# A planned order of an attention and FFN kernel: two units share one step of exponentials

## The chip, the cores and the metric

The kernel runs on one core of one Trainium2 chip. TensorE (PE) multiplies, VectorE (DVE), ScalarE (ACT) and GpSimd (POOL) do the rest, SyncE (SP) issues the DMAs. The metric is the time of one execution on the device, in microseconds, as the median of several runs.

## The reference, cut to what matters

```python
q, k, v: (8, 8, 576, 64); omega: (128, 64); w_in: (512, 2048); w_out: (2048, 512)
def phi(x):                                   # x is q or k, scaled by 64 ** -0.25
    h = x @ omega.T - sum(x * x) / 2
    return exp(h - max(h, axis=-1)) / sqrt(128)
kv  = einsum('bhsm,bhsd->bhmd', phi(k), v);  z = phi(k).sum(axis=2)
att = einsum('bhsm,bhmd->bhsd', phi(q), kv) / (einsum('bhsm,bhm->bhs', phi(q), z) + 1e-6)
x   = att.transpose(0, 2, 1, 3).reshape(4608, 512)
h   = x @ w_in
out = (0.5 * h * (1 + erf(h / sqrt(2)))) @ w_out
```

## The kernel before

**Units.** Attention is cut into 32 units: batch b (0 to 7) and a pair of heads j (0 to 3), unit number 4b + j. A unit projects its k and q (2 x 576 rows of each, 18 tiles of 128 columns: tiles 0 to 8 are k's, 9 to 17 q's), subtracts maxima, takes exp, forms the product of exp(k) with v (`kv`, or `kv_split`), brings exp(q) into the transposed form and divides (`num`, `den`, `rcp`, `div`). There are three kinds. Units 0 to 3 (mode 0) take exp tile by tile out of PSUM, with the maxima as a bias (`exp_tiles`). Units 4 to 7 (mode 1) subtract the maxima on DVE into an array of 128x2304 fp32 in SBUF (`shift_tiles`) and take one exp over it (`exps`). Units 8 to 31 (mode 2, "split") project in fp32r with high and low parts (`x_high` on ACT, `x_low` on POOL, `proj` and `proj_q` on PE, `proj_add` and `q_blocks` on DVE), subtract, and take one exp over the array too. A unit of modes 0 and 1 multiplies in fp32.

**The step of exponentials.** A split unit's step is one exp over 2304 columns, then a gelu of a single element. That gelu makes ACT load gelu's table back at once, since the gelus of the FFN follow; so a step has two loads of tables. There are two such arrays, `et` and `et2`. Split units with an even number above 8 use `et2`, all others of modes 1 and 2 `et`, so successive units take turns. What is written before the step is `split_pre`, what follows it `split_post`. In the order's list an option `pair`, 0 in this kernel, lets a unit on `et2` take the next unit with it.

**The FFN** works on 13 blocks of tokens (256, 256, ten of 384, 256). Block 0 is in fp32. Later blocks split x, the weights and the gelus into fp16 high and low parts, three products for one (`mm1`, `mm2`); from block 4 on the first product uses seven products of sums of quarter blocks in place of eight (`w_prod`), the second `w_mm2`. The weights are loaded as 16 pieces (w_in first), rounded (`w_hi`, `w_lo`, `w_shift`, `w_round`), their absolute maximum is taken (`w_abs` on ACT, `w_max` on DVE), and when the maximum of all of w_in is known (`wchain_a` to `wchain_f`, with two small products on PE, L559 and L565) they are scaled and split. The raw pieces have two buffers. PSUM has eight banks: three for accumulators of the second product, five shared by attention and the first product.

**Products of zeros.** At the start PE runs 22 products of zeros (`warm`), and eight groups of four more (`hold`, L448) stand in the order at places of their own.

**The order.** `op(engine, cost, function, ...)` notes every operation with what it reads and writes. ORDER is a list written out by a search, of numbers of operations with letters for the PSUM banks that each takes; `Planner.run` issues them in this order, and every engine keeps its own part of it strictly. So an engine that waits holds all that is behind it in its queue, SP's loads too.

Of the kernel before, what the change touches and what calls it, by code (L numbers as in the profile page):

```python
# [19 lines left out]
P = 128  # L20
# [8 lines left out]
X = dict(plain=8, kvp=8, eb0=8, ttr=1, pair=0, amax=63, qm=1, xm=0, km=0, prelu=1, n0=4, vs=5,  # L29
# [5 lines left out]
14 0 1 15 49 2a 12 17caa 50 22g 18 52dfa 57b 19 20 9h 4e 21 11 23 55 5e 24 58 59 56 7c 159 25hg 16 28 160 29 26 51 60ec 161  # L35
27 30aa 53 35ha 6b 3f 165 61 119 63 84 86 39f 54 85 31 64 62 65ga 70ba 162 166 40 37c 36 72f 38 71 66 167 87ada 32 73 168 90
120 92h 41cg 93 88 74b 94 67 42 43 75 95hf 163 89 44 122eba 96 171 123 169 33 657 91 172 45ca 98 8d 177 46 97 47 100ga 127h
48 76ca 101 174 99 34 105fa 128 173 658 125 107g 124 178 77 129 179 126 10d 78 106 130dh 108 79 80ec 180 175 68 133 131 81
170 181 121 660baa 132 164 82 183 663 83 661 109f 135ga 665c 664 110 662 184 666 186 176 189 667 111df 112 668cb 136 69 102
134 113 140ga 190 669 191 144a 185 693 142e 114 145 659 192 115hd 671 187 195 143 670 672 103 141 673 146ge 116 117 137 193  # L40
118 196 198 147 679aa 680 674ca 104 148 197 199 149 188 138 696baa 675 699 182 150gh 681c 201 139 300a 301 302 202 204 203
# [12 lines left out]
999 786 996a 1004 392 1000 393 417 527 409 429 1005 988 992 801 530b 997 656 394 1009 967 789b 802 528 405 397 531 432 1010
790 803 993 435 529 436 1001b 1006c 998 804 1002 1011aa 1013 532 536a 1012 1014 1007 1017 437 276 537 533 438 805 968 972
1003 439 277 395 538 534 539 535 793ab 794 795 540 542c 544b 545 806 543b 550 970 442 440 541 546 441 444 969 1021 807 445
796 552a 551 448 553 1018 554 809 443 811 1022 1008 547 1073 548 555 449 549 446 1015c 1019b 1075 556 1023a 450 560b 447 974
557 558 561 1080 398 451 1016 1024 452 971 1020 562 563 559 568a 566 564 569 565 797ca 453 1076 567 1081 570 576b 813 1025
454 574 577 1026 1085 1027 1028 461 457 973 571 810 455 578 798 1029 456 812 1030 572 575 975 582 459 579 580 573 1031 1032
976 799 583 1033 462 584a 1086 585 586 590 1036 581 977 458 800 460 591 1040 587 1707 1074 598 1059 588 592b 593 1037 594 399  # L60
1038 595 1077ba 1044 1042 1078 1041 1090 1039 1045 463 589 599 1082c 596 1043 464 1091 1095 1087a 1079 1083 1088 597 1100 465
1101 606 600a 1084 978 466 601 602 979 1092b 608b 1096 1089 1062 607 603 1164 1093 1104 980 1097c 1102aa 604 1094 605 1108
609 610 981 614 1105 1112 1098 1109 616a 1113 467 1034 1099 611 1103 617 618 1035 472 1110c 1106a 1111 1114b 612 615 815 1166
1116 622 613 1167 619 1115 1107 1046caa 1060 620 1171 468 1047 624b 1048 623 1176 625 1049 1117 470 1050 621 1172 1051 1168aa
1173b 1169 1118 474 626 1181 630 1174 396 1177 631 638 469 1052 1170 814 632a 1119 1178a 1709 1053 1175 1186 1165 471 1182
627 1056 1120 1183c 633 634 639 628 1061 1187 1125 629 1191 475 1179 1054 1184 1195 473 640b 641 1255 635 1192 1180 1063
1188a 1121 636 1193ba 1199 1189 476 1055 1185 1203 642 816 477 637 646 647 648 643 478 1122 1200 1204 1190 1194 1123 817a
1201a 644 645 1202 818 479 1196 1124 649 1064 650 1126 819 1129 1130 1205a 820 1206 1197c 1257 653 485 823b 1133 1135 1127
1065ab 1131 480 1258 1198 824 486 821 1066 825 822 651 1150 829a 481 826 487 835a 1262 1267 1128 1067 1134 827 1068 1208 836c
1263 830 483 1136 831 654 1209 1259aa 828 1069cb 1057 1132 1272 484 837b 832 838b 482 1268 844 1153 839 1260 488 489 490 1261  # L70
491 840 1207 1070 1151 1256 1137aaa 1071 1154 1138 1139 833 841 1072 1140 842 845 1141 1264c 1210 834 1269b 847a 1277 1708
1142 1143 1273 1265 848 1211 1282 1270 1271 1144 1212 1278 1147 1266 1145 849 843 850 1148 1283 1710 1721 846 1274b 1279c
1213 1214 1284aa 851 1286 1287 1275 856b 1285 853 1276 854 855 492 862 1280 852 1290 1291 1288b 1281 1152 1292c 1294 1293
1215 1295 863 864 1146 857 1058 1723 1289 1218 493 871 1296b 1219 1156ca 858 498 1724 1157 859 1155 860 872 1216 1297 1298
865a 1158 1711 873 866 1728 1220 1299 1159 867 496 1226 1725ba 652 1300 861 1301 1726 494 1160ac 874b 1733 868 1217 1224 1225
875 1302 876 1221 1738 1149 1222 1727 1712 1228baa 1303 1229 1304 880 1223 500 881 869 495 497 501 877 1722 870 1230 1305 882
1161 1231 502 1162 889 883a 1227 878 1729 1163 890 1734 884 808 1306 1232 1313 879 891 885 1311 1241 1730c 1233 1735a 892b
886 1234 1235 1315 1731 1314 499 1743 887 898 1316 1244 1748 1739 1309 1236 899 1736 888 1238 1307 503 893 894 1317 895 1732
896 1740b 1737 900 1310 897 901a 1308 1744 504 1237 1239 505 1749 1741 1242 1752 1750ca 1742 1745a 1312 507 902 903 910b 1751
904 907 1753 1756 1746 1318 1319baa 1320 1757 1245 1321 905 1747 911 1812 1322 1243 1323 1760 906 1754c 1324 1814 1758a 912  # L80
1325 908 1326 1761 1764 1815 1755 909 1759 1247cb 1246 1819 1762a 913 1763 1240 916 919a 917 1248 509 1249 920 914 1765 1250
1816aa 921 918 1766 1329 915 1330 925 928b 1820 1331 508 506 926 929 1817 1824 1251bc 1346 1347 1713 1818 1821a 922 1332 930
923 1825 927 924 511 1348 937a 934 1252 655 1327 1822 1335 1349 1333 1350 510 1714 1513 935 931 1829 1253 936 1715 1767 1351
1823 1352 938 943 932 939 1813 1254 1830 944 1336 1334 1354 1834 940 1716 933 1826b 1831c 945 1356 946b 1717 1768 1328 1769
947 952 941 1718 1827 1355 948 1832 1833 1357 1338ca 1514 953 954 1540 1358 1839 1828 1719 1840 949 942 512 1835 955 1770
1337 1339 1340 950 1836b 956 1720 1837 951 1362a 957 1515 1341 1838 958 1360 1843 1841ca 1847 1359 1842 1361 1342ab 1512 961
1851 1363 1343 1773 1364 964 1368b 1844 1369 1903 1771 959 1365 962 960 1517 1852 1344 1345 1370 1366 1367 2257 1774 1853a
1518 1848 1849b 1530 1516 1845c 1374a 1380a 1375 1850 1371 1372 1519 1381c 1905 1373 965 1376 1906 1854 1846 1526 1382b 1772
# [224 lines left out]
def favor_attention_ffn(ctx: ExitStack, tc: tile.TileContext, qT, kT, v, omT, w_in, w_out, out):  # L313
# [519 lines left out]
    def unit_plain(u):  # L833
# [24 lines left out]
        if u.mode == 1:  # L858
            op('ACT', 2.14, exps, u, w=ke + qe, tab='e')
# [779 lines left out]
```

## Time and profile before

| | |
|---|---|
| median of 3 runs | 947.71 us (947.4 to 949.87) |
| the profiled execution | 944.7 us, its span 942.9 us |
| PE, PE's weight loads | busy 930.0 us (99%), 665.1 us (71%) |
| DVE, ACT, POOL | busy 750.5 (80%), 771.3 (82%), 483.5 us (51%) |
| DMA | 71.11 MB, mean 75 GB/s; 250 to 330 GB/s in the first 30 us |
| granted clock of PE | 1.00 throughout |

Busy time is the time in which an engine has at least one instruction in flight; PE's products overlap, so their durations add up to more than it. The span is from the first instruction's start to the last one's end. Idle time of an engine is counted just before the instruction that ends it, with what released it.

### The profile page before, as it was taken

What the parts mean: (1) busy time and instruction counts of PE and PEld (TensorE: products, weight loads), DVE (VectorE), ACT (ScalarE), POOL (GpSimd) and SP (SyncE); (2) the same over time, 40 slices, a digit from 0 to 9 for tenths busy, and PEclk for the clock granted to TensorE, in tenths of its full rate; (3) what the DMA queues carried; (4) which work ended last, traced back from release to release, by engine and by line L of the source; (5) the groups of instructions that cost most, each with busy time, mean ns of one, the idle gap of its engine ahead of it and who ended that gap; (6) DMA issues with size and microseconds to landing.
All of it is one profiled execution on the core that took longest, in us unless ns stands there. A gap on an engine that the chain in (4) does not pass through costs nothing.

```text
span 942.9 us, 20416 instructions
## 1 busy us (share of the span) xinstructions
PE 930.0 (99%) x7324; PEld 665.1 (71%) x7324; DVE 750.5 (80%) x2021; ACT 771.3 (82%) x1662; POOL 483.5 (51%) x682
## 2 busy tenths in 40 slices
PE   9899999999999999999999999999999999999998
PEld 7666666666656677777867777777777767776776
DVE  4978999999988999899998999898988766542231
ACT  7979878899789889998899999999698866654443
POOL 2566237886668747775658755664465422040000
PEclk9999999999999999999999999999999999999999
DMA  9886231421122222213204222222112000000000
GB/s 276 258 259 202 63 102 57 114 76 44 59 78 65 88 78 61 73 55 91 73 13 108 74 75 61 68 62 63 51 52 86 1 1 34 2 12 24 1 35 24
DMA packets 46293, 71.11 MB, mean 75 GB/s; under 512 B 13680, under 2 KB 22256, under 8 KB 46192
## 3 DMA queue, kind: packets, MB, share of 16 engines
q1 hardware_dynamic: 46192, 69.81, 25.6%
q8 instruction: 58, 0.95, 0.4%
q14 instruction: 43, 0.35, 0.1%
HBM read 60.36 MB, written 9.44 MB: 74 GB/s over the span
## 4 chain that ended last, share of the span: by engine, by line
PE 80%; DVE 8%; ACT 8%; issue 2%; DMA 1%; POOL 1%; ACTq 0%; SPq 0%; DVEq 0%; POOLq 0%
PE p L1406 21%; PE p L1504 8%; PE p L1506 8%; PE p L1505 8%; PE p L1193 8%; PE p L1188 3%; PE p L764 3%; PE p L1214 3%; PE p L1217 3%; PE p L1219 3%; PE p L1218 3%; PE p L902 2%; PE p L924 2%; PE p L1006 2%; PE p L755 2%
## 5 line engine op out<-in xcount | busy, mean ns | idle before, releaser
L894 POOL TENSOR_TENSOR r<-xt,r 64x288 fp32r<-64x288 f32 (+2 forms) x216 | 170.2, 798 | 162.9 <-ACT r L885 115.4
L1504 PE MATMUL p<-woh,gh 128*128 128x512 f16 (+1 forms) x432 | 161.0, 373 | 0.0
L1505 PE MATMUL p<-woh,gl 128*128 128x512 f16 (+1 forms) x432 | 160.3, 371 | 0.1
L1506 PE MATMUL p<-wol,gh 128*128 128x512 f16 (+1 forms) x432 | 160.3, 371 | 0.0
L1406 PEld LDWEIGHTS <-w 128*128 128x128 f16 x1728 | 139.6, 98 | 20.2 <-issue 0.7
L1406 PE MATMUL p<-xh,w 128*128 128x192 f16 (+1 forms) x1152 | 147.9, 243 | 0.1
L1406 PE MATMUL p<-xl,w 128*128 128x192 f16 (+1 forms) x576 | 137.3, 243 | 0.0
L1406 PE MATMUL p<-xh,wih 128*128 128x192 f16 (+1 forms) x432 | 103.3, 243 | 0.0
L1406 PE MATMUL p<-xl,wih 128*128 128x192 f16 (+1 forms) x432 | 103.0, 243 | 0.1
L1406 PE MATMUL p<-xh,wil 128*128 128x192 f16 (+1 forms) x432 | 103.0, 243 | 0.0
L1431 ACT ACTIVATE p<-p,bs 128x384 f32<-128x384 f32 (+1 forms) x108 | 58.0, 539 | 52.9 <-PE p L1406 52.7
L885 ACT CAST r<-xt 128x256 fp32r<-128x256 f32 (+2 forms) x216 | 85.3, 405 | 5.9 <-PE p L924 1.7
L1406 PEld LDWEIGHTS <-wih 128*128 128x128 f16 x864 | 78.5, 98 | 8.3 <-issue 0.2
L1506 PEld LDWEIGHTS <-gh 128*128 128x128 f16 x432 | 42.3, 98 | 47.3
L1440 DVE SCALAR_TENSOR_TENSOR gl<-p,bs,gh 128x384 f16<-128x384 f32 (+1 forms) x108 | 63.3, 595 | 15.3 <-ACT gh L1437 13.6
L1504 PEld LDWEIGHTS <-gh 128*128 128x128 f16 x432 | 42.1, 97 | 28.0
L1437 ACT ACTIVATE gh<-p,bs 128x384 f16<-128x384 f32 (+1 forms) x108 | 60.5, 568 | 1.2
L1505 PEld LDWEIGHTS <-gl 128*128 128x128 f16 x432 | 42.4, 98 | 24.8 <-DVE gl L1440 0.7
L1193 PE MATMUL p<-xl,wih 128*128 128x384 f16 (+1 forms) x192 | 59.3, 309 | 0.6 <-DVE xl L1182 0.6
L1193 PE MATMUL p<-xh,wih 128*128 128x384 f16 (+1 forms) x192 | 59.2, 309 | 0.4 <-DVE gl L1209 0.3
L1193 PE MATMUL p<-xh,wil 128*128 128x384 f16 (+1 forms) x192 | 59.2, 308 | 0.0
L775 ACT ACTIVATE dt<-p,vsc 64x288 f32<-64x288 f32 x96 | 47.6, 495 | 7.0 <-PE p L764 4.5
(238 smaller groups left out, 2574.8 us busy)
## 6 DMA issues: line engine op xcount, KB each, us to landing
xt<-in_kT SPq DMA_DIRECT2D x56, 288.0 KB, 4.0
xt<-in_qT SPq DMA_DIRECT2D x56, 288.0 KB, 3.9
out_x<-o SPq DMA_DIRECT2D x35, 256.0 KB, 2.3
raw<-in_w_in SPq DMA_DIRECT2D x16, 512.0 KB, 5.7
raw<-in_w_out SPq DMA_DIRECT2D x16, 512.0 KB, 4.4
w<-in_v SPq DMA_DIRECT2D x24, 320.0 KB, 4.0
vt<-in_v SPq DMA_DIRECT2D x8, 320.0 KB, 6.0
out_x<-o SPq DMA_DIRECT2D x2, 128.0 KB, 1.7
```

Of the source, the lines that this page charges most:

```text
L764: nc.tensor.matmul(ps[:, 0:HS], a[:, hh], c, start=(i == 0), stop=(i == len(ops) - 1))
L775: nc.scalar.activation(dt[r], ps, AF.Identity, bias=G['vsc', u.b][r, 1:2])
L885: nc.scalar.copy(G['r', u, x][:, 0:b - a], xf[:, a:b])
L894: nc.gpsimd.tensor_tensor(r, xf[D:, a:b], r, op=ALU.subtract)
L1193: nc.tensor.matmul(h[:, 0:t], w, (G['xh', n, j], G['xh', n, j], G['xl', n, j])[k][:, 0:t], start=(i == 0), stop=(i == 3 * NJ - 1))
L1406: nc.tensor.matmul(b[:, g * h:(g + 1) * h], w, x[:, kt], start=first and k == 0, stop=last and k == 6 * GP - 1, skip_group_check=True)
L1431: nc.scalar.activation(h, h, AF.Gelu, scale=G['bs', n][:, 2:3])
L1437: nc.scalar.activation(c_dst('gh', n, q, part), c_in(n, q, part), AF.Copy, scale=G['bs', n][:, 3:4])
L1440: nc.vector.scalar_tensor_tensor(c_dst('gl', n, q, part), c_in(n, q, part), G['bs', n][:, 3:4], c_dst('gh', n, q, part), op0=ALU.mult, op1 ...
L1504: nc.tensor.matmul(acc, gh, woh[:, c, c0:c1], start=begin, stop=False)
L1505: nc.tensor.matmul(acc, gl, woh[:, c, c0:c1], start=False, stop=False)
L1506: nc.tensor.matmul(acc, gh, wol[:, c, c0:c1], start=False, stop=end)
```

## The change

Three things change. `pair` is 1: units 10 and 11, 12 and 13, up to 30 and 31, are planned together, both `split_pre`, then one `exps` for the two with one load of each table and one dummy gelu, then both `split_post`; units 8 and 9 keep a step each. Units 4 to 7 take their exp in two steps (`exps_half`), k's nine tiles and q's nine. ORDER is another list, found anew for these operations. The tests of `u.mode` and `u.b`, and `u.et` for `et` in `shift_tiles`, name the same units and the same array as before.

```diff
-X = dict(plain=8, kvp=8, eb0=8, ttr=1, pair=0, amax=63, ...
+X = dict(plain=8, kvp=8, eb0=8, ttr=1, pair=1, amax=63, ...
-            u.mode = 0 if b == 0 else 1 if u.k < X['plain'] else 2
+            u.mode = 0 if u.k < 4 else 1 if u.k < X['plain'] else 2
...
-        nc.vector.tensor_tensor(et[:, ts], pv, G['nm', u][:, ts].unsqueeze(2).broadcast_to([P, n, M]), op=ALU.add)
+        nc.vector.tensor_tensor(u.et[:, ts], pv, G['nm', u][:, ts].unsqueeze(2).broadcast_to([P, n, M]), op=ALU.add)
...
+    def exps_half(u, s):
+        t = u.et[:, s * NT:(s + 1) * NT]
+        nc.scalar.activation(t, t, AF.Exp)
...
-        ring = ANY if u.mode == 0 else AT
+        ring = ANY if u.b == 0 else AT
...
         if u.mode == 1:
-            op('ACT', 2.14, exps, u, w=ke + qe, tab='e')
+            op('ACT', 1.07, exps_half, u, 0, w=ke, tab='e')
+            op('ACT', 1.07, exps_half, u, 1, w=qe, tab='e')
```

The whole of ORDER is replaced. Read with the names of the operations, PE's part has 1505 steps in both lists. Its stretch from unit 2's first quotient on reads, with the number of the unit:

```
before  num_plain(2,0) pair(4,1) q_trans(3) x3 num_plain(2,1) num_plain(3,0) q_trans(4,0) kv(4) pair(5,0) num_plain(3,1)
after   num_plain(2,0) q_trans(3) x3 pair(4,1) num_plain(2,1) num_plain(3,0) q_trans(4,0) kv(4) pair(5,0) num_plain(3,1)
```

ACT's part around it, where w_abs(i) is the maximum of piece i of w_in:

```
before  den(1,1) w_abs(1) exp_tiles(3) w_abs(0) q_copy(2) w_hi w_abs(2) den(2,0) bound exp_tiles(3) w_hi w_lo q_copy(3) x3 exps(4) den(2,1) bound w_hi den(3,0)
after   den(1,1) w_abs(0) q_copy(2) w_hi exp_tiles(3) q_copy(2) x2 exp_tiles(3) w_abs(1) den(2,0) q_copy(3) bound q_copy(3) w_hi w_lo q_copy(3) half(4,k) w_abs(2) den(2,1) half(4,q) den(3,0)
```

The loads between w_in's sixth piece and w_out's first are, on SP: before, unit 5's k, unit 4's v, w_in's last two pieces; after, unit 4's v, unit 5's k and v, w_in's last two pieces, unit 6's q, unit 5's q. The eight groups of zeros stand among PE's first 34 steps before, among its first 22 after.

## Rows read from the trace of the kernel before

**Rows 1.** The page: the span; busy us, share of the span, instructions.

```profile
span 942.9 us, 20416 instructions
...
PE 930.0 (99%) x7324; PEld 665.1 (71%) x7324; DVE 750.5 (80%) x2021; ACT 771.3 (82%) x1662; POOL 483.5 (51%) x682
```

**Rows 2.** Windows by stage: length, busy us of each engine, clock, DMA share, GB/s.

```profile
0.00:41.00 41.00, 38.75 (x377) 30.28 (x377) 26.51 (x71) 34.25 (x97) 13.90 (x15) 1.00 0.94 272
41.00:54.00 13.00, 9.30 (x87) 6.89 (x87) 10.35 (x31) 12.63 (x25) 8.54 (x6) 1.00 0.70 206
54.00:150.00 96.00, 96.00 (x550) 64.92 (x547) 84.40 (x188) 79.16 (x144) 46.38 (x53) 1.00 0.49 149
150.00:350.00 200.00, 197.84 (x1289) 125.26 (x1287) 183.54 (x520) 177.65 (x398) 146.37 (x207) 1.00 0.24 68
350.00:650.00 300.00, 298.45 (x2505) 224.05 (x2503) 276.48 (x797) 281.27 (x605) 190.42 (x277) 1.00 0.25 67
650.00:939.00 289.00, 289.00 (x2523) 213.42 (x2522) 169.23 (x419) 185.49 (x397) 77.93 (x125) 1.00 0.10 30
```

**Rows 3.** The chain that ended last: start us, us, what.

```profile
341.39 1.98 PE p L1406 x24
```

**Rows 4.** Waits of PE: total us, times, longest.

```profile
PE p L1006 <- DVE et L927: 1.1, 1, 1.1
```

**Rows 5.** Groups of ACT by line: busy us, mean ns, idle before.

```profile
L698 ACT ACTIVATE et<-et,kln 128x2304 f32<-128x2304 f32 x13 | 28.8, 2218 | 0.2
...
L700 ACT ACT_TABLE_LOAD x24 | 30.8, 1283 | 0.4
...
L495 ACT ACTIVATE raw<-raw 128x1024 f32<-128x1024 f32 x16 | 19.1, 1192 | 0.5 <-DMA raw<-in_w_out 0.2 <-DMA raw<-in_w_in 0.2
...
L698 ACT ACTIVATE et<-et 128x2304 f32<-128x2304 f32 x4 | 8.5, 2125 | 1.1 <-DVE et L694 1.1
...
L700 ACT ACTIVATE wmax<-wmax 1x1 f32<-1x1 f32 x24 | 4.9, 202 | 0.3
```

**Rows 6.** Windows of 7.2 us from each of the 24 split steps.

```profile
158.30:165.50 7.20, 7.20 (x51) 4.90 (x49) 6.61 (x20) 7.12 (x11) 6.22 (x10) 1.00 0.01 2
...
sum 172.80, PE 172.48 PEld 120.98 DVE 149.68 ACT 169.87 POOL 104.88; mean PE 7.19 PEld 5.04 DVE 6.24 ACT 7.08 POOL 4.37
```

**Rows 7.** Timeline of PE, 38 to 56 us: start, us, instruction, idle before.

```profile
41.45 1.16 PE L673 MATMUL p<-om,xt 64*128 64x128 f32 x16 [1.05 <-DVE et L694]
...
45.99 1.19 PE L755 MATMUL p<-w 128*64 128x288 f32 x8 [1.13 <-ACT w L749]
48.49 0.66 PE L745 MATMUL p<-ident,et 128*128 128x128 f32 x4 [1.31 <-ACT et L698]
...
53.07 1.19 PE L755 MATMUL p<-w 128*64 128x288 f32 x8 [0.82 <-DVE xa L810]
```

**Rows 8.** Timeline of ACT, 39 to 47 us.

```profile
39.96 1.23 ACT L519 ACTIVATE w<-w 128x1024 f32<-128x1024 f32 x1
...
41.39 1.32 ACT L689 ACTIVATE w<-p,nm 128x128 f32<-128x128 f32 x4
```

**Rows 9.** Timeline of DVE, 41 to 64 us.

```profile
43.79 0.70 DVE L506 TENSOR_SCALAR w<-raw 128x1024 int32<-128x1024 int32 x1
...
45.00 1.28 DVE L694 TENSOR_TENSOR et<-p,nm 128x512 f32<-128x512 f32 x2
...
60.37 0.15 DVE L556 TENSOR_REDUCE wcm<-wmax 128x1 f32<-128x8 f32 x1
```

**Rows 10.** Timeline of PE near 62 and near 485 us.

```profile
59.76 2.11 PE L1188 MATMUL p<-xa,w 128*128 128x256 f32 x9
61.70 0.27 PE L559 MATMUL p<-ident,wcm 128*1 128x128 f32 x1
...
484.77 0.48 PE L764 MATMUL p<-qh,kvh 128*128 128x288 f32 x1
485.09 0.29 PE L764 MATMUL p<-qh,kvl 128*128 128x288 f32 x1
```

More of the change, by code (lines that the diff above doesn't have):

```diff
@@ L27 @@
 TBS = (256, 256) + (384,) * 10 + (256,)
-X = dict(plain=8, kvp=8, eb0=8, ttr=1, pair=0, amax=63, qm=1, xm=0, km=0, prelu=1, n0=4, vs=5,
+X = dict(plain=8, kvp=8, eb0=8, ttr=1, pair=1, amax=63, qm=1, xm=0, km=0, prelu=1, n0=4, vs=5,
          tx=4, ss=4, xh=8, gh=3, xp=0, qs=1431655680, kl=572662272, wl=21845, wg=0, px=0)
 ORDER = """
-14 0 1 15 49 2a 12 17caa 50 22g 18 52dfa 57b 19 20 9h 4e 21 11 23 55 5e 24 58 59 56 7c 159 25hg 16 28 160 29 26 51 60ec 161
-27 30aa 53 35ha 6b 3f 165 61 119 63 84 86 39f 54 85 31 64 62 65ga 70ba 162 166 40 37c 36 72f 38 71 66 167 87ada 32 73 168 90
@@ L37 @@
[L37 to L41, printed above, removed]
@@ new lines @@
+3176 3088 2214 3522 2236 2237 2650 3091 2224 2225 2652 2630ab 3171 2631 2238 2239 2240 2218 2226 2644 2241 2223 2660a 1705
+2219 2227 2632 2649 2242 2633 3181 2243 2806 2651 2645 2653 3089 2244 3115 2661b 2245 2248 3092 3094 3096 2249 2250 3093
+2662c 3172ca 3095 3173 3097 3185 3174 3177b 3178 2663 3100 3098 3186 3179 3099 2664 3116 3101 2665 3102caa 3131 2654 2656
+3103 3104 3133 3190 3105 2093 3106 3182b 2666 3191 3107 3195 3139 3183 2655 2657 2670 3108 3219 3109 3187c 3196 3118 2246
+3188 3184 3132 2658 2251 3192b 3117 3189 2675 3193 3199 2659 3203 2667 3112 3200 3197ca 3204 3194 3207 2668 3208 2671 3198
@@ new lines @@
+4601 4570 4183b 4182 4206 4166 4599 4593 4168 4571 4612 4161 4572 4594 4207 4184a 4613 4185c 4162 4614 4208 4169 4187 4615
+4186 4600 4209 4189 4170 4604bc 4210 4602 4616 4190 4191 4188 4603 4605 4211 4606 4212 4193 4617 4618 4198 4607 4624 4213
+4192 4194 4608cb 4609 4199 4214 4610 4625 4611 4215 4784 4626 4216 4621 4195 4217 4622 4202 4218 4196 4203 4197 4623 4219
+4204 4627 4200 4205 4638a 4639b 4628 4220 4640d 4201 4221 4222 4629 4642 4630 4632 4223 4071 4785 4634 4631 4636 4226 4641
+4644 4633 4227 4787 4645 4635 4637 4228 4643 4648 4653 4224 4791 4229 4649 4657 4658 4232 4646 4233 4661e 4650 4651 4647
@@ L233 @@
+4870 4890 4878 4891 4871 4845 4874 4892 4893 4846 4894 4882 4898c 4895 4875 4879 4896 4872 4897 4883 4779 4880 4876 4921
+4899a 4900e 4901 4881 4902 4903 4884 4877 4885 4904 4922 4908 4905 4923 4924 4906 4913 4925 4914 4909 4926 4927 4915 4917
+4910 4928 4929 4930 4931 4918 4907 4932 4933 4916 4911 4934 4912 4919 4920 4935 4936 4939 4937 4940 4941 4942 4938 4943 4944
+4945 4948 4946 4947 4949 4950
 """
@@ L836, in unit_plain @@
         op('SP', 0, load_v, u, r=['vt1s'], w=[u.vk], size=327e3)
-        nm, ring = ('nm', u), ANY if u.mode == 0 else AT
+        nm, ring = ('nm', u), ANY if u.b == 0 else AT
         tiles = []
```

372 lines of the change are left out of this document (184 added, 188 removed), and 3 rows, old and new, of the table ORDER.

## The prediction

> **What bounds the kernel now.** I read the page's head first: TensorE (PE) is busy 930.0 of 942.9 us, ScalarE (ACT) 82%, VectorE (DVE) 80% [rows 1]. [...]
>
> The windows by stage say where that idle time is [rows 2]: 2.25 us before 41 us (about one of it the start), 3.70 from 41 to 54, none to 150, 2.16 from 150 to 350, 1.55 from 350 to 650, none from there to 939; what is left, 3.3 us, is the tail of the last store. So 9.7 us lie between the start and the tail. In the stage where the pairs work, 150 to 650 us, PE has 3.7 us idle in 500, although ACT is busy 459 of these and DVE 460. The reader is to see that a 90% engine beside a 99% engine bounds nothing by itself.
>
> The view of waits says who ends PE's idle time. ACT ends two of the early waits, 1.13 and 1.31 us [rows 7]; the largest of the middle, 1.1 us, ends with a transpose on DVE [rows 4]. So what ACT holds back in sight is 2.4 us, and it is early, away from the pairs.
>
> **The change part by part.**
>
> *The pairs.* Each of the 24 split units now costs ACT a load of exp's table, 2304 columns of exp in 2.218 us, a load of gelu's table, and a dummy gelu of 0.202; a load is 1.283 [rows 5]. Units 8 and 9 stay alone and 22 units become 11 pairs, so 11 times two loads and one dummy go: 11 x (2 x 1.283 + 0.202) = 30.4 us of ACT. A step of a pair holds ACT for 2 x 1.283 + 2 x 2.218 + 0.202 = 7.2 us at a stretch, where a single one holds it for 5.0. On the path this saves nothing in itself: 24 windows of 7.2 us, each from the start of a step of before, have 0.32 us of PE's idle time in 172.8 [rows 6]. That is also the best row for the cost of the longer block, since the windows reach 2.2 us past the step. But in those 2.2 us ACT had begun to serve what stood behind the step: copies of projections that free PSUM banks, gelus that PE's second products need. Bounds: nothing per step, or the whole second exp, 2.22 us, which is 24.4 us over 11 steps. The windows are nearer to nothing: I take 0.2 us for all.
>
> A pair also fills both buffers of exponents before either is emptied, where single units took turns. DVE and GpSimd then work in larger lumps. No row prices that; its effect comes through the same stalls and is inside these bounds.
>
> *The halves.* Units 4 to 7 take exp in two steps of 1152 columns. Between 1024 columns in 1.192 us and 2304 in 2.125 [rows 5] lies 1.29, so two cost 2.57, 0.45 more; four units 1.8 us of ACT. So ACT's balance is 28.6 us less work, 4% of 771. For units 5 to 7 a shorter wait is worth nothing: PE is busy 96.00 of 96.00 us from 54 to 150 [rows 2]. For unit 4 PE asks first for its transposes, which need the second half, in both orders. What the halves give is that the first one can run while DVE still shifts the second.
>
> *The early order.* Here I follow PE [rows 7]. It waits 1.05 us before the second projection of unit 4. The new order puts unit 3's transposes in that place. They need unit 3's last exps, at 41.39 to 42.71 [rows 8]; ACT now has two maxima of w_in (1.23 us for the one just ahead) and a denominator behind them, so they end near 39.8 and PE, free at 40.4, does not wait. Their copies come as much earlier, and the 1.13 us of the product of unit 3 goes too. Next is unit 4: its second projection ends where it did, 42.6; on DVE its maxima and shifts follow, which ended at 46.28, with a shift of weights of 0.70 between that now stands before them: 45.6 [rows 9]. The second half takes 1.29: PE goes on at about 46.95 for 48.49, 1.55 us sooner. The 0.82 us at 53.07 waited for the division of unit 3, whose denominators now follow the half at once: gone too. Together 2.35 us (the waits of 1.05 and 1.13 are inside it, since unit 4 sets the pace after them).
>
> What is late next is the scale of w_in. Its transpose on PE starts at 61.70 behind a maximum that DVE ends at 60.5 [rows 9, 10]. The products of block 0's fourth chunk, which ran just before it from about 60.0, stand behind it in the new order, 1.7 us less of PE's work ahead of it, so PE would be there at 61.7 - 1.7 - 2.35 = 57.65; the maximum, with two DVE steps of unit 5 now behind it (its start at 60.37 would be the end of the pieces' maxima, about 59.2), can be there near 59.3. PE would wait 1.65 us and keep 0.7. The order of loads brings one v earlier and two loads of unit 5 and 6 ahead of w_out's first piece, which can take more. Bounds 0 and 2.35; I take 1.0, a little above what the scale leaves, since DVE and ACT reach it earlier too.
>
> *The zeros.* Both orders hold eight groups of four products of zeros. They stand earlier now. What hides them is PE's wait for q, k and the first exps: even with them PE has 2.25 us idle before 41 us [rows 2]. Without that cover they would cost as much after as before. Nothing.
>
> *The middle.* Idle 2.16 + 1.55 = 3.7 us [rows 2]. The order is new everywhere, and no row tells which waits it keeps. Bounds 0 and 3.7; a third, 1.2, since PE's waits there end with DVE and GpSimd too, whose work is the same.
>
> *What PE pays more.* The first product of a group in fp32r took 0.48 us, the next 0.29 [rows 10]: 0.19 for the change of type. The new order has 171 such groups for 167: 0.7 us. The numbers of products are the same.
>
> **The sum.** 942.9 - 1.0 - 1.2 + 0.7 + 0.2 = 941.6 us of span. The profiled execution took 944.7, 1.8 above its span, and the median of the runs is 947.7, 3.0 above that. So 941.6 + 1.8 + 3.0 = 946.4 us, 0.14% less. A measurement of this kernel can tell about 0.3%, 2.8 us, from no change: this is no change.
>
> [...] Weight loads are busy 71% here [rows 1]. [...]
>
> **The rivals.**
>
> *Faster by more than 0.3%.* The slack of 28.6 us on ACT lets the new order lose most of the waits: 2.35 early and all 3.7 of the middle, less the 0.7 for types: 947.7 - 5.35 = 942.4. For it: DVE's late transposes follow projections that wait for ACT's casts, so part of DVE's waits is ACT's. Against: DVE works 460 us of the same 500, as before. It decides when more than 2.8 + 0.7 = 3.5 of these 6.05 us are won.
>
> *Slower: a pair's step starves PE.* ACT serves nothing for 7.2 us, and PE's three or five free PSUM banks are full before it ends. For it: ACT is busy 281.27 of 300 us from 350 to 650 [rows 2], so what stood behind comes late as a whole. Against: [rows 6]. To be slower by 0.3% a step must stall PE by (2.8 + 1.3) / 11 = 0.37 us; at half a us, 11 x 0.5 = 5.5, less what the forecast wins: 951.7. At half of the second exp, 958.4.
>
> *PE is not the bound at all.* PE's products, though busy, stretch to ACT's pace, and ACT's 28.6 us come out whole: 947.7 - 28.6 = 919.1. [...]
>
> **The numbers.** No measurable change 0.46, faster through the order 0.32, slower through the steps 0.20, ACT's bound 0.02. So faster 0.34, same 0.46, slower 0.20. The range: the faster case reaches down to 941 or so, with all 9.7 us between start and tail won 938.7; the slower one up to 958. 940.5 to 952 leaves some 0.05 below and 0.1 above. The likeliest case alone, with its bounds (early 0 to 2.35, middle 0 to 3.7, types 0.7, up to 0.25 us per step), spans 944.9 to 950.5, cut by what counts as no change.
>
> **What would show it.** ACT: 29 loads on the lines of the steps for 51, busy about 740 us. Windows of 7.2 us from the start of each pair's step: PE idle under 0.1 us each; if it is over 0.37, the slower rival is right. From 41 to 54 PE idle 1.5 to 2.5 us for 3.70, and a new wait at the transpose of w_in's maximum near 58 us: if it is not there, the early gain is whole. From 150 to 650 PE idle 2 to 4 us. The forecast is wrong if PE loses over 5 us there, or if it is idle between 54 and 150, where w_out's pieces or the scale come too late.

## The result and the profile after

The changed kernel takes 953.34 us in the median of four executions beside 947.56 for before: a ratio of 1.0059, 95% interval 1.0038 to 1.0080. Ten executions in two comparisons have the same median; the second comparison gave 1.0059 again (1.0039 to 1.0078). It is slower by 0.6%, 5.8 us, where 946.4 us was forecast.

The page of the profiled execution (953.23 us, span 951.4), its head and the line of the granted clock, answers to [rows 1]:

```profile
span 951.4 us, 20473 instructions
PE 936.1 (98%) x7324; PEld 668.9 (70%) x7324; DVE 752.9 (79%) x2021; ACT 744.8 (78%) x1633; POOL 483.5 (51%) x682
PEclk9989999999999999999999999999999999999999
```

ScalarE (ACT) has lost nearly what was counted out for it, 26.5 us of 28.6: 744.8 us busy, "about 740" forecast, and 29 loads of tables on the steps' lines. The span is 8.5 us longer all the same, and in its third slice there is a dip of the clock that before does not show. The two longest waits of PE are new [rows 4]; ACT's is before unit 4's transposes, DVE's at 430.87 us, before a product of block 5:

```profile
PE p L749 <- ACT et L704: 2.8, 1, 2.8
PE p L1411 <- DVE gl L1445: 1.4, 1, 1.4
```

The windows by stage, with the short stretch of that dip as the last row, answer to [rows 2]; after the bounds of a window come its length, then the busy time of PE, of its weight loads (PEld), DVE, ACT and POOL, the granted clock, and DMA's share and GB/s:

```profile
0.00:41.00 41.00, 39.48 (x377) 30.78 (x377) 25.71 (x67) 33.57 (x98) 14.95 (x16) 1.00 0.91 266
41.00:54.00 13.00, 9.39 (x69) 7.33 (x65) 11.32 (x32) 12.61 (x24) 6.58 (x5) 0.87 0.98 275
54.00:150.00 96.00, 95.88 (x538) 64.68 (x539) 83.97 (x183) 76.59 (x139) 44.39 (x49) 0.98 0.45 141
150.00:350.00 200.00, 199.32 (x1316) 127.34 (x1314) 180.61 (x523) 173.96 (x394) 150.10 (x216) 1.00 0.26 68
350.00:650.00 300.00, 294.59 (x2437) 219.31 (x2438) 276.88 (x781) 260.42 (x577) 188.50 (x270) 1.00 0.26 69
...
50.59:57.42 6.83, 6.83 (x40) 5.62 (x39) 4.77 (x14) 6.81 (x12) 4.13 (x3) 0.50 0.78 254
```

Two stages are worse. From 41 to 54 us PE is idle 3.61 us, hardly less than before, and then works 6.83 us at a granted clock of 0.50. From 350 to 650 it is idle 5.41 us for 1.55; from 150 to 350 it has gained, 0.68 for 2.16. PE's timeline shows how the early part went, and answers to [rows 7]:

```profile
42.98 0.65 PE L749 MATMUL p<-ident,w 128*128 128x128 f32 x4 [0.84 <-ACT w L753]
43.56 1.16 PE L673 MATMUL p<-om,xt 64*128 64x128 f32 x16
...
49.74 0.66 PE L749 MATMUL p<-ident,et 128*128 128x128 f32 x4 [2.77 <-ACT et L704]
50.24 3.72 PE L711 MATMUL p<-vt,et 128*128 128x65 f32 x18
```

The transposes of unit 4 (49.74) start 1.25 us later than in before, not 1.5 sooner, after 2.77 us in one piece in which PE does nothing. The product behind them took 3.72 us, and 2.17 where the clock stayed up (experiment 2).

To see where the rest went, one execution is laid on the other by PE's order: each operation of PE counts the start-to-start time that the quickest fifth of its kind has in the trace of before (zeros count nothing), and at equal counts ("us of PE work") the start times are compared. This is worked out from the traces, for the kernels below too; the kinds' times are an estimate, so a few tenths of a us say nothing:

```
us later than the profiled before, at us of PE work
              30    60   130   160   320   360   400   410   450   560   600   end
changed      0.8   3.9   4.1   2.3   1.5   3.5   2.9   4.4   8.2   6.2   8.1   8.1
filled       1.0   1.8   1.9   0.2  -0.6   2.1   1.5   3.0   6.8   5.1   7.0   7.0
before_filled 0.1  0.2   0.2   0.2   0.2   0.2   0.3   0.3   0.3   2.2   2.2   2.2
short_steps  0.9   1.6   1.8   0.1  -0.6   3.4   2.7   4.2   8.0   5.9   7.4   7.0
no_low       0.5   1.3   1.5  -0.3  -1.1   2.3   1.6   2.2   5.5   3.4   5.3   5.3
pieces_filled 0.9  1.6   1.8   0.0   1.0   3.9   3.3   3.5   7.3   5.9   6.7   6.7
late_before  0.9   1.7   1.8   0.1  -0.6   2.4   2.5   2.5   2.7   2.6   2.6   2.6
```

The changed kernel loses 3 us early, wins 1.8 at 130 to 160, loses 2.0 at 320 to 360, and 5.3 between 400 and 450 (about 422 to 474 us of its time). Of the 5.3, 2.0 come back by 560. From 420 to 475 us PE is idle 2.95 us, where before has none in the same stretch (417 to 467); the rest is time in which PE counts as busy, or an error of the estimate. At 422 us PE works in block 5, and the pair of units 18 and 19 takes its step at 432.9.

One thing has to be known to read every median here: in some executions of either kernel the mean granted clock of TensorE is 0.994 to 0.996, and in some 0.998 to 1.000; in the profile above, at 0.996, it is 0.50 for a stretch and 1.00 before and behind it ("half clock" and "full clock" below). Of 109 executions of before in five comparisons, 46 have a mean granted clock of 0.996 or less and a median of 949.96 us, 46 have 0.999 or more and 946.66, and 17 lie between at 0.998 and 947.56. Of ten of the changed kernel, six stand at or below 0.996 (953.9) and four at or above 0.998 (952.0). Kernels of different comparisons are set against each other below; the before at 0.999 or more takes 946.3 to 946.9 us in these five, so a difference of under 0.6 us between two comparisons says nothing.

### The profile page after: what moved, and what is told of

Read it like the earlier page. It is cut to its first block, busy times and chain, and to the rows that moved or that the text cites. A ratio compares the mean times of both kernels' runs of the same rounds, so it can differ in the third digit from the quotient of the medians.

```text
span 951.4 us, 20473 instructions
## 1 busy us (share of the span) xinstructions
PE 936.1 (98%) x7324; PEld 668.9 (70%) x7324; DVE 752.9 (79%) x2021; ACT 744.8 (78%) x1633; POOL 483.5 (51%) x682
## 4 chain that ended last, share of the span: by engine, by line
PE 83%; DVE 7%; ACT 6%; issue 2%; DMA 1%; POOL 0%; ACTq 0%; DVEq 0%; POOLq 0%
PE p L1411 21%; PE p L1198 8%; PE p L1509 8%; PE p L1510 8%; PE p L1511 8%; PE p L768 3%; PE p L1222 3%; PE p L1224 3%; PE p L1223 3%; PE p L1193 3%; PE p L1219 3%; PE p L907 3%; PE p L929 2%; PE p L1011 2%; DMA xt<-in_kT 1%
## 5 line engine op out<-in xcount | busy, mean ns | idle before, releaser
L899 POOL TENSOR_TENSOR r<-xt,r 64x288 fp32r<-64x288 f32 (+2 forms) x216 | 172.4, 809 | 138.6 <-ACT r L890 87.2
L1445 DVE SCALAR_TENSOR_TENSOR gl<-p,bs,gh 128x384 f16<-128x384 f32 (+1 forms) x108 | 63.6, 595 | 30.4 <-ACT gh L1442 29.6
```

What stands on the lines that cost most here:

```text
L899: nc.gpsimd.tensor_tensor(r, xf[D:, a:b], r, op=ALU.subtract)
L1445: nc.vector.scalar_tensor_tensor(c_dst('gl', n, q, part), c_in(n, q, part), G['bs', n][:, 3:4], c_dst('gh', n, q, part), op0=ALU.mult, op1 ...
```

## The experiments

Theories: **A**, the early wait and the half clock behind it; **B**, the pairs' long steps on ACT; **C**, VectorE (DVE) instructions held up by GpSimd (POOL); **D**, the searched order itself; later **E**, a form of D: a pair packs the next pair's projections. All kernels hold the operations in one written order, so an order can be taken from before up to one entry and from the changed kernel behind it.

**1. early_before.** The order of before to about 130 us of PE work, then the changed order:

```diff
 ORDER = """
-14 1 2b 15 0 12 17gea 49 20 18 52haa 22c ...
+14 0 1 15 49 2 12 17caa 50 22g 18 52dfa ...
```

> The order of before up to about 130 us of PE work (units 4 to 7 with their exponentials in one step again), then the changed order with its pairs. Theory A (early wait and clock): of the 5.8 us that the change lost, about 4.0 were lost before 80 us, at PE's wait of 2.77 us for the second half of unit 4's exponentials and in the 6.83 us at half clock behind it; then 953.3 - 4.0 = 949.3 us (ratio to before 1.002), no stretch at half clock and PE idle near 50 us of at most 1.3 us in one piece. Theory B (long steps): the loss comes from the eleven pairs' steps of 7.2 us, which this kernel keeps all; then about 953 us (1.006). Theory C (collisions of VectorE with GpSimd at 427 and 628 us): also about 953 us, unless the shifted times move a collision, which gives up to 3 us either way.

Measured: 951.49 us, 1.0038 (1.0020 to 1.0056). That is 1.9 less than the changed kernel, not 4.0. Nine of its twelve executions have a mean clock of 0.997 or more and a median of 951.4; the four of the changed kernel at 0.998 or more have 952.0, so at full clock the early order is worth about 0.6. Its own profiled execution has the half clock (mean 0.996; 0.85 from 41 to 54 us, 0.94 from 54 to 80), although the early order is that of before; PE's timeline there:

```profile
47.33 1.19 PE L761 MATMUL p<-w 128*64 128x288 f32 x8 [1.15 <-ACT w L755]
49.81 0.89 PE L751 MATMUL p<-ident,et 128*128 128x128 f32 x4 [1.29 <-ACT et L703]
50.49 4.05 PE L713 MATMUL p<-vt,et 128*128 128x65 f32 x18
```

Here a wait of 1.45 us at 42.76, then 1.15 and 1.29, were followed by half clock; in the profiled before 1.05, 1.13 and 1.31 [rows 7] were not. So the fall of the clock is not a property of the changed order alone.

**2. filled.** Six more groups of zeros where PE waits:

```diff
-    for i in range(8):
+    for i in range(14):
         op('PE', 0.43, hold, i, r=['z', ('w32', 0, NF - 1)], new=[(ANY, ('hold', i))])
...
 # ORDER, right ahead of q_trans(u4, 0)
+11f 12f 13f 14f 15f 16f
```

> The changed kernel with six more groups of products of zeros (24 matmuls of 256 columns, about 2.6 us) in PE's order right before the transposes of unit 4, where PE waits 2.77 us. They add work that nothing uses, in an idle gap. Theory A with the clock as the carrier: PE's wait there shrinks to 0.2 to 0.5 us, the granted clock stays at full speed from 50 to 58 us, and half of the 6.83 us comes back: 953.3 - 3.4 = 950 us (1.0025). If the wait itself is the loss and the slow clock only runs under other waits: 953.3 (1.006). Theories B and C: 953.3.

Measured: 952.17 us, 1.0040 (1.0024 to 1.0056); all twelve executions have a mean clock of 0.999 or more. PE's timeline and the two windows around it:

```profile
47.15 3.88 PE L447 MATMUL p<-w 128*128 128x256 bf16 x24
50.86 0.60 PE L751 MATMUL p<-ident,et 128*128 128x128 f32 x4
51.30 2.17 PE L713 MATMUL p<-vt,et 128*128 128x65 f32 x18
...
41.00:54.00 13.00, 11.91 (x103) 8.68 (x101) 12.05 (x34) 12.46 (x24) 6.63 (x5) 1.00 1.00 277
54.00:80.00 26.00, 26.00 (x146) 17.69 (x144) 21.91 (x46) 22.56 (x38) 14.53 (x12) 1.00 0.61 210
```

With work in the gap the granted clock stays at 1.00 and the product takes 2.17 us. But only 1.2 us of the median came back: it is 4.4 us above the before of that comparison (947.75), at full clock.

**3. before_filled.** The same remedy for before, seven groups in its three gaps (`2 + 2 + 3` zeros ahead of pair(u4, 1), num_plain(u3, 0) and q_trans(u4, 0)).

> The kernel before with seven more groups of products of zeros (28 matmuls of 256 columns, about 3 us) in three idle gaps of PE between 41 and 49 us (1.05, 1.13 and 1.31 us in the trace of before); they add work that nothing uses. Theory A (clock): of 29 executions of before, 16 had a mean granted clock of 0.998 or more and took 946.6 us in the median, 13 had 0.995 to 0.996 and took 950.7. If those 13 are executions in which the clock fell behind these gaps, all executions now stand at 0.998 or more and the median is 946.6 (ratio 0.998). If the clock falls elsewhere, the two groups stay and so does the median, 947.7.

Measured: 946.83 us, 0.9987 (0.9977 to 0.9998), all twelve executions at 1.00. This is what before takes at full clock (946.66), so the half clock of before goes with those gaps: of the 23 executions of before beside these twelve, nine stand at 0.996 or less. The clean comparison is filled against before_filled, both always at full clock: 952.17 - 946.83 = 5.3 us. The half clock explains next to nothing of the 5.8, since it strikes both kernels; what is left of theory A is the 0.6 us of experiment 1.

**4. filled_four.** Four groups in place of six, since 24 products took 3.88 us in a gap of 2.77; and **changed_again**, the changed kernel once more.

```diff
-11f 12f 13f 14f 15f 16f
+11f 12f 13f 14f
```

> The changed kernel with four groups of zeros (16 matmuls, 2.5 us at the 0.16 us that one took in the filled kernel) before unit 4's transposes. If the clock is what the wait costs: mean clock 0.999 or more in all executions and 952.2 - 1.1 = 951.1 us (1.0033), about 2.3 us below the changed kernel. If a gap of 0.3 us is left and the clock still falls in some executions: two groups of times 3 us apart.

> The changed kernel itself once more. From its four executions (three with a mean clock of 0.996 and 953.5 us, one with 0.998 and 952.2): 953.3 us (1.0059), most executions with the half-clock stretch; before has it in 13 of 29, 9 of 23 and 12 of 26 executions of the earlier comparisons.

Measured: 952.20 us, 1.0044 (1.0027 to 1.0061), all at 0.999 or more, with 0.29 us of the gap left; and 953.10, 1.0059 (1.0039 to 1.0078), three of six at 0.996 or below. Two groups fewer change nothing, so the expected 1.1 was wrong; the changed order at full clock is 952.2 either way.

**5. late_before.** Filled up to about 350 us of PE work, then the order of before, a step for each unit (mid_before likewise, with a third part):

```diff
 # ORDER: entries 1 to 2039 of the changed order, then
-the changed order's other entries
+what is left, as the order of before has it   (mid_before: up to its entry 3000, then the changed order again)
```

> The filled kernel (changed order, zeros before unit 4's transposes) up to about 350 us of PE work, and from there to the end the order of before with a step for each unit. In the profile of the filled kernel the lost time against before stands at +1 to +2 us at that point and at +7 at the end. Theories B and D (the loss is made behind 350 us): 952.2 - 5 = 947 us (ratio 0.9995). If the loss is made early: 952 (1.004).

Measured: 948.66 us, 1.0001 (0.9990 to 1.0013). 3.5 us of the 5.3 go with the later part. **mid_before** has the order of before only from 350 to 505:

> The changed order up to about 350 us of PE work, the order of before (each unit with a step of its own: units 16 to 21) up to about 505 us, then the changed order again. In the profile the changed kernel loses 3.3 to 8.1 = 4.8 us in this part. Theories B and C: 953.3 - 4.8 = 948.5 us (1.001); a loss put down to A alone leaves it at 953 (1.006).

Measured: 956.79 us, 1.0079 (1.0054 to 1.0105), against every theory. At the seam, where the orders meet again, PE waits for unit 20's division:

```profile
531.75 0.37 PE L770 MATMUL p<-qh,kvh 128*128 128x288 f32 x1 [3.50 <-DVE xsb L819]
```

Its profiled execution loses 6.3 us there, with 3.41 us at half clock right behind the wait (0.98 from 480 to 580 us), and all six executions have a mean clock of 0.996 or less. Between 400 and 450 us of PE work it loses 0.1 us, where the changed order loses 5.3. The total is inconclusive; that stretch, with late_before, says that the loss there belongs to the changed order.

**6. unpaired and pairs_alone.** The pairs taken apart within the changed order (the even unit's step moved ahead as far as its operands allow), and the pairs made within before's order (before_filled) with whatever must follow pushed behind. In these kernels a pair is two neighbouring entries of the order:

```diff
     def exps(u):
         nc.scalar.activation(u.et, u.et, AF.Exp, bias=kln)
-        if u.k not in (10, 12, 14, 16, 18, 20, 22, 24, 26, 28, 30):
-            nc.scalar.activation(wmax[0:1, 1, 0:1], wmax[0:1, 1, 0:1], AF.Gelu)
+        nc.scalar.activation(wmax[0:1, 1, 0:1], wmax[0:1, 1, 0:1], AF.Gelu)
...
 # ORDER of unpaired: exps(u10), exps(u12), ... moved up; of pairs_alone: exps(u10), exps(u12), ... moved down to exps(u11), exps(u13), ...
```

> The changed kernel with the six groups of zeros of the filled kernel (952.2 us), and the eleven pairs taken apart: the even unit's exponentials come where the order of before has them if they are ready then, otherwise right after their last operand, with a return of the tables to Gelu behind each unit. ScalarE gets 11 x 2.77 = 30.5 us more (two table loads of 1.283 and a dummy of 0.2 each). Theory B (the step of 7.2 us is the loss): the 3 to 5 us lost behind the pair at 433 us come back, 948 (1.001). Theory D (the searched order, not the length of a step, loses, and it uses the ScalarE time that the pairs save): part of the 30.5 us lands on PE, 957 to 980 us (1.01 to 1.034).

> Before_filled with the pairs and nothing else: the even unit's exponentials wait for the odd unit's, the order of before is kept, and whatever depends on the even unit comes as soon behind as it can. ScalarE is spared 30.5 us. If ScalarE's time or the table loads were what holds PE up, this is as fast as before or faster: 940 to 947 us. If before's order of PE is cut to single steps (theory D), PE stands at each pair until the odd unit's operands are there: 11 times 2 to 10 us, 970 to 1050 us (1.02 to 1.11).

Measured: 1007.88 us, 1.0628 (1.0604 to 1.0652), and 1068.82 us, 1.1285 (1.1252 to 1.1317), both beyond what was expected (their mean granted clocks are 0.98 and 0.94). PE's waits, the three largest of unpaired and the two largest of pairs_alone:

```profile
PE p L1511 <- ACT gh L1444: 12.5, 4, 3.5
PE p L1200 <- DVE gl L1216: 10.8, 4, 4.3
PE p L1413 <- ACT p L1423: 10.2, 3, 3.9
...
PE p L909 <- DVE nm L919: 23.1, 8, 6.7
PE p L1013 <- DVE nm L919: 9.7, 4, 5.5
```

Without the pairs the changed order waits for gelus and their operands, which ACT now serves later: the order has spent the 30 us that the pairs save. With pairs and no new order PE stands for sums of projections on DVE. Neither part can be priced alone. Taking the pairs apart does not win, as theory B had it, but the run adds 30 us of ACT as well and so does not decide about the steps' length; the next one does.

**7. short_steps.** Filled, with the odd unit's exponentials left out.

```diff
-        nc.scalar.activation(u.et, u.et, AF.Exp, bias=kln)
+        if u.k < 10 or u.k % 2 == 0:
+            nc.scalar.activation(u.et, u.et, AF.Exp, bias=kln)
```

> The filled kernel with the exponentials of the odd unit of each pair left out (the units 11, 13, ... 31 go on with the shifted products themselves), so that a pair's step takes 5.0 us of ScalarE in place of 7.2 in the same place of the same order. Theory B (the length of the step starves PE behind it): the 3.8 us lost behind the pair at 433 us shrink by at least the 2.2 us that the step is shorter, and likewise the smaller losses behind other pairs: 952.2 - 3 to - 6 = 946 to 949 us (1.000 or below). Theory D (the searched order's own arrangement of vector work and projections loses): within 1 us of 952.2 (1.0035 to 1.0045).

Measured: 951.20 us, 1.0039 (1.0026 to 1.0053): 24 us less of ACT and 1.0 us gained. Between 400 and 450 us of PE work it still loses 5.3, so theory B falls there. Behind the shorter step ACT itself stands waiting for PE:

```profile
438.70 0.56 ACT L1445 ACTIVATE gh<-p,bs 128x384 f16<-128x384 f32 x1
441.29 0.40 ACT L893 CAST r<-xt 128x256 fp32r<-128x256 f32 x1 [2.03 <-PE p L910]
```

**8. pieces, pieces_filled.** GpSimd's two long instructions for each unit in three pieces, in the changed kernel and in filled.

```diff
     def k_shift(u):
         es = u.et[:, 0:NT]
-        nc.gpsimd.tensor_tensor(es, es, G['nm', u][:, 0:NT].unsqueeze(2).broadcast_to([P, NT, M]), op=ALU.subtract if X['ttr'] else ALU.add)
+        for t in range(0, NT, 3):
+            nc.gpsimd.tensor_tensor(es[:, t:t + 3], es[:, t:t + 3], G['nm', u][:, t:t + 3].unsqueeze(2).broadcast_to([P, 3, M]), op=ALU.subtract)
...
```

> The changed kernel, with GpSimd's two long instructions of every split unit (the shift of K's products, and that of Q's where GpSimd has it, 2.1 us each) cut into three each. Theory C: a VectorE instruction that starts just behind a GpSimd instruction stands until that one ends, so the waits of PE at 430.9 us (1.36) and 630 us (1.1) and what follows them shrink to a third: 953.3 - 3 = 950 us (1.003). Theory B (the pairs' steps as such): no change, 953.3 (1.006). More instructions on GpSimd cost about 0.1 us for each, off PE's path.

> The filled kernel with GpSimd's long shifts in three pieces each. Of twelve executions of the pieces alone, the four at full clock took 949.2 us in the median, and the twelve of the filled kernel 952.2. Theory C (VectorE standing behind a whole GpSimd instruction): both gains together, 949.2 us (1.0015). If the pieces do nothing: 952.2 (1.0045).

Measured: 952.84 us, 1.0038 (1.0019 to 1.0056), and 951.44, 1.0037 (1.0024 to 1.0051). In its place the theory holds. DVE and POOL of the changed kernel, and of pieces_filled:

```profile
427.17 2.13 DVE L946 TENSOR_TENSOR nq<-mx,mc 32x36 f32<-32x36 f32 x1
...
427.14 2.11 POOL L925 TENSOR_TENSOR w<-w,nm 128x1152 f32<-128x1152 f32 x1
```

```profile
427.59 0.86 DVE L949 TENSOR_TENSOR nq<-mx,mc 32x36 f32<-32x36 f32 x1
...
427.58 1.61 POOL L928 TENSOR_TENSOR w<-w,nm 128x384 f32<-128x384 f32 x2
```

The DVE instruction of 36 columns lasts 2.13 us, as long as the GpSimd instruction of 2.11 us that began 0.03 us ahead of it; beside pieces of some 0.8 us it lasts 0.86. GpSimd's 36 long instructions, cut in three each, cost it 492.8 us busy for 483.5 in the changed kernel, 0.13 for each of the 72 more. From 400 to 410 us of PE work the loss falls from 1.5 to 0.3. But as a whole 0.7 us come of it: between 160 and 320 this kernel is 1.6 us worse than filled, and the 3.8 us between 410 and 450 stand untouched. Of the twelve executions of pieces, eight at 0.996 or less have a median of 953.1 and four at 0.998 or more 949.2, 2.8 below the changed kernel's four; pieces_filled, always at full clock, does not repeat that (951.4), and why is not known. Nor does the edit take the collisions away: 28 DVE instructions are still held up in pieces_filled, 16.4 us in all for 20.2 in filled. What theory C costs as a whole stays open.

**9. no_low.** Filled without GpSimd's subtraction for units 20 and 21.

```diff
     def x_low(u, x):
+        if u.k in (20, 21):
+            return
```

> The filled kernel without GpSimd's subtraction for the units 20 and 21 (the low part of their keys and queries is not computed; 18 instructions of 0.5 to 0.85 us). Theory E: a pair ties both product buffers to one step, so the projections of the next pair stand packed right behind it, and PE waits there for the chain copy on ScalarE, subtraction on GpSimd, projection: the waits of the weight loads on GpSimd at 444 to 452 us (0.25, 0.52, 0.90 and the ones beside them) go, and the 5.3 us lost at 400 to 450 us of PE work shrink to 2.5 to 3.5; in all 952.2 - 1.5 to - 2.5 = about 950 us (1.002 to 1.003). If the loss there has another cause: the same 5.3 and 952.2 (1.004).

Measured: 950.37 us, 1.0031 (1.0019 to 1.0044), 1.8 less than filled, as expected; but not as the theory says. From 410 to 450 us of PE work the loss falls from 3.8 to 3.3 only; 0.9 of the gain is at 400 to 410, where another DVE instruction is held, earlier and for 1.6 us, and costs PE less. What the weight loads waited for behind the pair, in the changed kernel (438 to 478 us) and then in no_low (436 to 476):

```profile
PEld p L929 <- issue: 1.5, 4, 0.6
PEld p L929 <- POOL r L899: 1.4, 2, 0.9
PEld L1011 <- DVE xsb L817: 0.8, 1, 0.8
PEld p L907 <- ACT kvs L1018: 0.3, 1, 0.3
```

```profile
PEld L1015 <- issue: 0.9, 1, 0.9
PEld p L933 <- ACT lo L915: 0.8, 2, 0.6
PEld p L933 <- ACT p L1440: 0.6, 1, 0.6
PEld p L911 <- ACT kvs L1022: 0.5, 1, 0.5
```

Without the waits for POOL, waits for ACT's copies stand at the same projections. In before, the same stretch of weight loads (430 to 470 us) has no wait that the view lists. So shortening GpSimd's link alone gives little. DVE's link no run shortened, and the chain that ended last says that it is the longer one. In the changed kernel, from 420 to 475 us, DVE makes up 18 us of this chain, PE 25, ACT 9; in before (417 to 467) it is PE alone; in short_steps (419 to 474) DVE still has 18, in no_low (419 to 473) 9. A part of it behind the pair, in which DVE forms the low part of unit 19's exponentials (L1000), transposes unit 20's q and takes its maxima (L932, L934), and does work for the FFN's gelus (L1445) and the maximum of unit 23's v (L1035):

```profile
446.44 0.81 DVE vt L1000
447.72 0.40 DVE w L932
448.14 0.45 DVE mx L934
...
450.92 0.53 DVE gl L1445
451.45 0.73 DVE vmax L1035
452.18 0.54 DVE gl L1445
452.86 0.51 PE p L929 x2
```

**10. halves_undone and halves_swapped.** Filled with the exponentials of units 4 to 7 in one instruction at the second half's place; and before_filled with halves, Q's first, and one group of zeros ahead of unit 4's transposes. In halves_undone the sums over K of units 5 and 7 stand ahead of that place in the order, so they are taken of the shifted products.

```diff
     def exps_half(u, s):
-        t = u.et[:, s * NT:(s + 1) * NT]
-        nc.scalar.activation(t, t, AF.Exp)
+        if s:
+            nc.scalar.activation(u.et, u.et, AF.Exp)
```

> The filled kernel with the exponentials of units 4 to 7 in one instruction again, at the place of the second half. If the halves gave what the forecast says (the Q half alone stands before unit 4's transposes): 952.2 + 1.0 = 953.2 us (1.0055), with PE held about 1 us longer before these transposes. If the first half only filled an idle ScalarE, nothing: 952.2 (1.0045).

> Before_filled (946.8 us) with the exponentials of units 4 to 7 in halves at the same place, Q's half first, and one group of zeros in place of three before unit 4's transposes. The transposes need Q's half alone, so they run beside the exponentials of K's half: the 1.3 us that PE stands there shrink by at most the transposes' 0.5 us and about 0.5 us of what is queued: 946.8 - 0.3 to - 0.8 = 946.2 us (0.998). [...]

Measured: 955.85 us, 1.0089 (1.0076 to 1.0102), 3.7 more than filled; and 946.74, 0.9988 (0.9977 to 0.9999), the same as before_filled. In the changed order, which was found for halves, taking them apart costs 3.7 us, and this shows at units 5 to 7: the loss grows from 1.4 to 4.8 us between 65 and 120 us of PE work. Of unit 4 the run tells nothing, since the zeros run to 50.5 us and hide the undivided exponentials (48.24 to 50.37). In before's order the halves are worth nothing: the wait ahead of unit 4's transposes is gone, but 1.21 us stand at 55.08 instead, ahead of unit 3's second quotient.

**11. joined, joined_pieces.** Before_filled with the changed order from about 130 to 293 us of PE work, where the changed kernel won; and the same with GpSimd's pieces.

```diff
 # ORDER: entries 1 to 640 of before, then
-what is left, as the order of before has it
+the changed order's entries up to 1683, then what is left, as the order of before has it
```

> The order of before to about 130 us of PE work with zeros in its three gaps, then the changed order to about 293 us (two pairs in it), then the order of before again: it keeps the stretch in which the changed kernel gained (1.8 us at 160 to 170 us of PE work in the profiles, 2.4 by 300) and leaves out those in which it lost. By the profiles 946.8 - 1.8 to - 2.4 = 944.4 to 945.0 us (0.997). If the gain was the chance of one profiled execution: 946.8 (0.9987).

> The joined kernel with GpSimd's long shifts in three pieces each. Theory C: each execution of before also has such collisions at changing places (1.8 us at 171 us in the trace of before, 1.7 at 524 us in that of before_filled), so 1 to 2 us less than the joined kernel: 943 to 944 us (0.9955). If the pieces only add GpSimd instructions: the same as the joined kernel or up to 1 us more.

Measured: 948.01 us, 0.9995 (0.9984 to 1.0006), and 948.87, 1.0010 (1.0001 to 1.0019). The 1.8 us were won again by 160, but about as much, some 1.5 each, was lost at the first seam and at the second. The fastest version found is before_filled (halves_swapped is equal), 0.13% below before.

## Why the prediction was wrong

**The pairs on ACT: right.** The 30 us that were counted, 22 loads and 11 dummies, are gone, and the sentence that this saves nothing in itself on the path holds: in short_steps another 24 us bring 1.0. That PE and not ACT sets the pace, which the forecast takes for granted, holds with it: 26.5 us less of ACT did not shorten the span.

**The step of 7.2 us: right in size.** 0.2 us was taken. The sum of the windows of 7.2 us from the eleven steps, as [rows 6]:

```profile
sum 79.20, PE 79.16 PEld 53.47 DVE 69.12 ACT 78.68 POOL 42.95; mean PE 7.20 PEld 4.86 DVE 6.28 ACT 7.15 POOL 3.90
```

PE is idle 0.04 us of 79.2. The slower rival, at 0.20, named the right side, but by a mechanism that the runs do not bear out: that its side came true is luck.

**The middle: the step that failed.** "The order is new everywhere, and no row tells which waits it keeps. Bounds 0 and 3.7; a third, 1.2": this bounded what a new order can win and gave it nothing that it can lose. From 350 to 650 us PE is idle 5.41 us for 1.55, and at full clock the changed order costs 5.3 us. With the order of before from there on, 3.5 us of these are gone (late_before). The prediction touched the place and passed on: a pair "also fills both buffers of exponents before either is emptied ... No row prices that". The trace of before had rows for it: its unit 20 has its first projection at 432.1 us, 25 us ahead of unit 19's sums over K, because one buffer is free while the other is still filled. In the changed kernel it comes at 440.8, 0.7 us after the pair's step ends. The nine projections of the eleven even units (10 to 30) are spread over 20.0 us each in before and 13.0 in the changed kernel (first start to last, mean).

Shown is that the changed order brings the loss, that most of it lies in the stretch around the pair of units 18 and 19, and that neither the step's length nor GpSimd's subtraction alone makes it. That the packed projections make it is not shown, and one thing speaks against it as the whole cause: they are packed behind every pair. By the table's method, in the 25 us behind a step the changed kernel loses 2.6 us at 432.9, 0.9 and 0.6 at 330.0 and 588.2, and behind the other eight it loses nothing or wins up to 1.0; behind six of them PE alone makes up the chain that ended last. Why it is this pair, and whether less work on DVE or more time for these projections would give the loss back, stays open: there is no third buffer, and moving the projections alone moves the work of three other engines. Of the 5.3 us at 400 to 450, 1.5 are the held DVE instruction, which is no part of the packing.

**The early order: -1.0 taken, none came.** The step that failed is "45.6". DVE's shifts of unit 4 ended at 48.5, since in the new order unit 4's second projection runs at 43.56, behind a copy by ACT (0.84 us of PE's wait), and a division, a shift of weights and two short steps of unit 3's bound stood beside the maxima before the shifts. The second half followed at 48.53 to 49.69. At full clock the early part loses a little: 0.9 from 30 to 130 us of PE work in filled, 0.6 by early_before. No wait near 58 us came, because PE was late itself.

**The halves.** "For units 5 to 7 a shorter wait is worth nothing" was read from before's order and does not carry over to the new one, where taking the halves apart costs 3.7 us there. In before's order unit 4 gains nothing by them as a whole; in the new one that was not measured.

**The clock** was in no term. It costs before 3.3 us (949.96 - 946.66) in 46 of 109 executions and the changed kernel 1.9 (953.9 - 952.0) in six of ten, so it is 0.5 us or less of the difference of the medians (5.8, and 5.3 at full clock). The two profiled executions, one with and one without, make it look like 3 of 8.5. The profiled before was also one of its quickest.

**Zeros and changes of type** were not tested by themselves. The price of 0.19 us for a change of type is one pair of rows. Over the traces the first fp32r product of `num` behind a product of another type holds the next one back for 0.27 us in before and 0.24 in the changed kernel (medians), and 0.13 behind one of its own type, so four more groups cost some 0.5 us, not 0.7.

## What to carry to other kernels

What a reordered program can lose is not bounded by zero. Where two units share a step, look in the old trace at how early the next user of each buffer starts, and at which engines its work will then meet; here that shows which work comes packed, though not at which pair it costs. Compare profiled executions only where their clocks agree, and fill gaps of the engine ahead of a dense stretch if they let its clock fall; here that was the only clean gain (946.83 us for 947.94). When two parts of a change were fitted to each other, undoing one (1.063) or doing one (1.129) tells that they need each other, not what either is worth.

## What the runs showed of the hardware

TensorE's granted clock fell to 0.50 for 6.83 us behind a gap of 2.77 us without work in the changed kernel (some 10.2 us around a gap of 2.80 in a second profile of it, by its 0.81 from 41 to 54 us and 0.56 from 54 to 60), and in early_before for 6.83 us around gaps of 1.45, 1.15 and 1.29 us with products between them. In the profiled before, gaps of 1.05, 1.13 and 1.31 us were not followed by a fall. It stayed up in the 12, 12 and 7 executions of the three kernels with zeros in these gaps (filled, before_filled, filled_four: mean clock 0.999 or more).

Some DVE instructions were held until a GpSimd instruction ended. In the changed kernel 1136 DVE instructions start within a running GpSimd instruction, and 28 took over 0.4 us more than the median of their kind (the same line, operation, tiles and shape; 20.6 us in all; in before 18, 12.0 us). These end at most one usual duration after the other does. In filled and filled_four it is the same instructions (27 and 28). Of the DVE instructions that start with over 0.4 us of a GpSimd instruction still to run, those with two SBUF inputs are held by over 0.25 us in 34 of 41 cases (before: 29 of 41), all others in 1 of 475 (before: 0 of 525). Why it is these is not shown.
